# A fused attention and gated feed-forward kernel: early transposes moved to TensorE, loads reordered, one exp phase moved forward, wider weight reads

## The chip, the cores and the metric

The kernel runs on one core of one Trainium2 chip. The metric is device time in microseconds (us). Executions of one kernel agree within about 1%, some are longer; those over 1.5% above the fastest are marked slow. A profile is one execution; its span is about 2 us shorter than the device time of the same execution.

PE is the matrix engine (TensorE), which writes its results to a memory of its own, PSUM; PEld is its weight loads, DVE the vector engine, ACT the scalar engine (exp, log, sine), POOL issues the loads from memory, SP the DMA transposes and the stores.

## The reference

```python
q, k, v: (8, 8, 576, 64)   p: (8, 8, 32, 64)   w_in: (512, 2048)   w_out: (2048, 512)
def sm_attn(qq, kk, vv):                       # softmax(scale * qq kk^T) vv
p_packed = sm_attn(p, k, v)                    # 32 packed rows per batch and head
out = sm_attn(q, p_packed, p_packed)
x = out.transpose(0, 2, 1, 3).reshape(4608, 512)
h = x @ w_in;  y = (h * cos(h)) @ w_out        # y is the result, float32
```

## The kernel before

The kernel works batch by batch, in a software pipeline. For batch `b` there are these pieces, each with its name in the profile:

- `s1` (matmul of transposed k against p), its exp on ACT, and `pp` (packed values); `s2` (transposed q), its exp, `sums` and `normalise` (result `a2n`);
- `ppw`: the packed values times `w_in`, kept as `PPW`; then h (`hT`, with the 64 rows left over of each batch in `ht`), its cosine on ACT (`cosT`), the product on DVE (`gT`, `joint`);
- the output matmuls `ot`, which serve as filler for PE while ACT and DVE work.

Slot `s` of the main loop does h of batch `s`, the output of batch `s-1`, and attention for `s+1` and `s+2`. ACT needs one function table for exp and log and another for sine (1.28 us for each switch), so the exps of a slot are gathered into one exp phase. The parts that the argument touches:

```python
    def load(n, b):                                  # from memory, cast to bf16
        t = x[n, b] = ld_pool.tile([KP, H, KC * D], BF16, ...)
        G.dma_start(out=t, in_=src[n][b].rearrange("h (p c) d -> p h (c d)", c=KC))
    def dma_T(n, b):                                 # transpose by DMA
        t, f = T_tile(n, b)
        nc.sync.dma_start_transpose(out=t, in_=f)
    def pe_T(n, b, engs):                            # transpose by PE, copied out of PSUM
        t, f = T_tile(n, b)
        for i in range(3):
            ps = work.tile([128, 8, KP], BF16, name="tps", tag="w")
            for j in range(8):
                nc.tensor.transpose(ps[:, j, :], f[:, (8*i+j)*128:(8*i+j+1)*128], ident[0:KP, 0:KP])
            copy(engs[i % len(engs)], t[:, 8*i:8*i+8, :], ps)
    # ... (cut)
    # loads in program order: k0 v0 q0, w_in (512 columns), w_in (the rest), p, w_out x4,
    #                         k1 q1 v1, k2 q2 v2
    # ... batch 0 by pe_T: s1, pp, s2, ppw, sums, normalise
    dma_T("k", 1)
    dma_T("q", 1)
    for fc in range(NFC):                            # slot 0: h of batch 0, nothing else
        if fc % 4 == 2 and fc < 12:
            ppw_piece(0, fc // 4 + 1, [V, A])
        h_mm(0, fc)
        run(h_sin(0, fc))
    dup_p(2, 16, V); pack_p(1, 4); pack_p(4, 8)
    dma_T("k", 2)
    set_filler(0)                                    # middle phase: attention of batches 1 and 2
    exp_table()
    fill(16)                                         # 16 output matmuls of batch 0
    for i in range(3): s1_mm(1, i); s1_exp(1, i)
    fill(12)
    pp_piece(1)
    # ... s2(1), ppw(1), s1(2), sums(1), normalise(1), pp(2), 16 more output matmuls
    for s in range(1, B):                            # slots 1 to 7
        # ... load(s+2); dma_T("k", s+2); h in two halves with an exp phase between; dma_T("q", s+2)
```

The softmax here doesn't subtract the row's maximum and nothing guards it: scores larger than these inputs give would overflow.

Of the kernel before, what the change touches and what calls it, by code (L numbers as in the profile page):

```python
# [8 lines left out]
FP32 = mybir.dt.float32  # L9
# [7 lines left out]
def kernel(  # L17
# [54 lines left out]
    a1T = const.tile([KP, KC, 2, 4, 32], BF16, name="a1T")  # L72
    src = {"k": k, "q": q, "v": v}
# [16 lines left out]
    def copy(eng, out, in_):  # L90
        if eng is A:
            A.copy(out=out, in_=in_)  # L92
        else:
            eng.tensor_copy(out=out, in_=in_)  # L94


    def T_tile(n, b):
        t = xT[n, b] = T_pool.tile([128, H * KC // 2, KP], BF16, name=n + "T", tag=n + "T")
        return t, x[n, b].rearrange("p h x -> p (h x)")
# [5 lines left out]
    def pe_T(n, b, engs):  # L105
        t, f = T_tile(n, b)
        for i in range(3):
            ps = work.tile([128, 8, KP], BF16, name="tps", tag="w")
            for j in range(8):
                nc.tensor.transpose(ps[:, j, :], f[:, (8 * i + j) * 128:(8 * i + j + 1) * 128], ident[0:KP, 0:KP])  # L110
            copy(engs[i % len(engs)], t[:, 8 * i:8 * i + 8, :], ps)

# [17 lines left out]
    def s1_mm(b, i):  # L130

        ps = s1_ps[b, i] = work.tile([KP, 2, 2, 4, 32], FP32, name="s1", tag="w")
        for h in range(H):
            nc.tensor.matmul(ps[:, :, h % 2, h // 2, :], xT["k", b][:, h * (KC // 2) + i, :],  # L134
                             P2[:, b, h], start=True, stop=True)

    def s1_exp(b, i):
        ps = s1_ps.pop((b, i))
        A.activation(out=a1T[:, 2 * i:2 * i + 2].rearrange("p c o a n -> p (c o a n)"),  # L139
                     in_=ps.rearrange("p c o a n -> p (c o a n)"), func=AF.Exp, scale=scale)  # L140
# [23 lines left out]
    def ppw_piece(b, n, engs):  # L164
        if b not in PPW:
            PPW[b] = ppw_pool.tile([128, 2, DF], BF16, name="PPW", tag="PPW")
        ps = [work.tile([128, 512], FP32, name="ppw", tag="w") for _ in range(2)]
        for hp in range(4):
            for o in range(2):
                r = slice(64 * o, 64 * o + 64)  # L170
                nc.tensor.matmul(ps[o][32 * hp:32 * hp + 32], ppT[b][r, 2 * hp + o, :],  # L171
                                 w_in_bf[r, hp, n * 512:(n + 1) * 512], start=True, stop=True,
                                 tile_position=(64 * o, 32 * hp))
        for g in range(2):
            dst = PPW[b][:, g, n * 512:(n + 1) * 512]
            s = rinv[b][:, 2 * g:2 * g + 1]
            if engs[g] is A:
                A.activation(out=dst, in_=ps[g], func=AF.Copy, scale=s)  # L178
            else:
                engs[g].tensor_scalar(out=dst, in0=ps[g], scalar1=s, scalar2=None, op0=ALU.mult)  # L180

    def s2_mm(b, g):

        ps = s2_ps[b, g] = [work.tile([128, S // 2], FP32, name="s2", tag="w") for _ in range(2)]
        for hp in range(4):
            for o in range(2):
                r = slice(64 * o, 64 * o + 64)
                h = 2 * hp + g
                nc.tensor.matmul(ps[o][32 * hp:32 * hp + 32], ppT[b][r, h, :],
                                 xT["q", b][r, 3 * h:3 * h + 3, :].rearrange("p c t -> p (c t)"),  # L190
                                 start=True, stop=True, tile_position=(64 * o, 32 * hp))
# [114 lines left out]
    def run(todo):  # L306
        for f in todo:
            f()
# [3 lines left out]
    nc.sync.dma_start(out=p_raw[:, 0:2, :], in_=p_rows[:, 0:2, :])  # L312
# [4 lines left out]
    load_w_in(512, DF)  # L317
    G.dma_start(out=p_raw[:, 2:, :], in_=p_rows[:, 2:, :])
    for n in range(4):
        load_w_out(n)  # L320
    for b in (1, 2):
        for n in "kqv":
            load(n, b)
    exp_table()
    V.memset(P2[:, 0], 0.0)
# [4 lines left out]
    for j in range(4):  # L330
        V.memset(ones_blk[j * 32:(j + 1) * 32, j * 32:(j + 1) * 32], 1.0)

    def dup_p(a, b, eng):
        for t in range(2):
            eng.tensor_copy(out=p_bf[:, a:b, t, :], in_=p_raw[:, a:b, :])

    dup_p(0, 2, V)
    pack_p(0, 1)
# [5 lines left out]
    V.memset(P2[:, 1:], 0.0)  # L344
# [4 lines left out]
    ppw_piece(0, 0, [V, V])  # L349
    for i in range(3):  # L350
        sums(0, i)
    normalise(0)
    dma_T("k", 1)
    dma_T("q", 1)


    for fc in range(NFC):
        if fc % 4 == 2 and fc < 12:
            ppw_piece(0, fc // 4 + 1, [V, A])
        h_mm(0, fc)  # L360
        run(h_sin(0, fc))
    dup_p(2, 16, V)
    pack_p(1, 4)
    pack_p(4, 8)
    dma_T("k", 2)


    set_filler(0)
    exp_table()
    fill(16)  # L370
# [3 lines left out]
    fill(12)  # L374
    pp_piece(1)
    for g in range(2):
        s2_mm(1, g)
        s2_exp(1, g)
    ppw_piece(1, 0, [V, V])
    fill(4)  # L380
    for i in range(3):
        s1_mm(2, i)
        s1_exp(2, i)
        sums(1, i)
        fill(2)
    normalise(1)
    dma_T("q", 2)
    for n in range(1, 4):
        ppw_piece(1, n, [V, A])
        fill(2)  # L390
    pp_piece(2)
    for n in "kqv":
        load(n, 3)
# [16 lines left out]
    def exp_phase(s, b2, b1):  # L410
        exp_table()
        s2_exp(b2, 0)
        s2_mm(b2, 1)
        s2_exp(b2, 1)
        fill(3)
        for i in range(3):
            if b1 is not None:
                s1_mm(b1, i)
                s1_exp(b1, i)
            fill(4)  # L420
        for i in range(3):
            sums(b2, i)
            fill(2)
        normalise(b2)
        h_mm(s, 8)
        fill(3)
        h_mm(s, 9)
        fill(3)

    for s in range(1, B):  # L430
        if s > 1:
            set_filler(s - 1)
        n1, n2 = s + 1 < B, s + 2 < B
        if s > 1 and n2:
            for n in "kqv":
                load(n, s + 2)
        if n2:
            dma_T("k", s + 2)
        before = {}
        if n1:  # L440
            before[1] = [lambda: ppw_piece(s + 1, 0, [V, A])]
            before[3] = [lambda: ppw_piece(s + 1, 1, [V, A])]
            before[7] = [lambda: s2_mm(s + 1, 0)]
            before[11] = [lambda: ppw_piece(s + 1, 2, [V, A])]
            before[13] = [lambda: ppw_piece(s + 1, 3, [V, A])]
        if n2:
            before[9] = [lambda: pp_piece(s + 2)]
        rest = filler[1] - (27 if n1 else 0)
        h_steps(s, range(0, 8), before, rest // 2)
        if n1:  # L450
            exp_phase(s, s + 1, s + 2 if n2 else None)
        if n2:
            dma_T("q", s + 2)
        h_steps(s, range(8, 16), before, filler[1])
        fill(100)
# [32 lines left out]
```

## Time and profile before

| | us |
|---|---|
| device time, median of 3 (range) | 290.17 (289.23 to 291.49) |
| the profiled execution, marked slow | 299.3, span 297.1 |

The first view is the table of windows of the kernel before: the stretch in us from the span's start, its length, then the busy time of each engine with its number of instructions, PE's granted clock (1 is full), the DMA share and GB/s.

```profile
core 0: us, PE busy (x) PEld busy (x) DVE busy (x) ACT busy (x) POOL busy (x), PEclk, DMA share, GB/s
40.00:110.00 70.00, 48.55 (x492) 24.59 (x500) 27.16 (x52) 33.11 (x55) 5.37 (x7) 0.76 1.30 161
110.00:160.00 50.00, 48.88 (x469) 25.73 (x475) 29.74 (x49) 40.99 (x66) 4.60 (x6) 1.00 0.90 150
160.00:220.00 60.00, 59.19 (x567) 31.57 (x573) 39.07 (x70) 48.35 (x78) 1.53 (x2) 1.00 0.57 103
220.00:280.00 60.00, 59.48 (x383) 29.63 (x390) 37.22 (x57) 41.18 (x64) 0.00 (x0) 1.00 0.19 49
```

From 110 us on PE is busy 98 to 99% of the time at full clock: this part is bound by PE. From 40 to 110 us PE is busy 48.55 of 70 us at a mean clock of 0.76, ACT is not even half busy, and the DMA share is 1.30. The start is bound by something else. The chain of waits (the work that ended last, followed back from the end), by engine and by line, says what:

```profile
PE 65%; DMA 30%; ACT 1%; issue 1%; POOL 1%; DVE 1%; POOLq 0%; ACTq 0%
PE ot L280 38%; DMA kT<-k_bf 19%; PE hT L235 15%; DMA k_bf<-in_k_dram 8%; DMA q_bf<-in_q_dram 3%; PE ppw L171 3%; PE ht L242 2%; PE pp L148 1%; PE sm L208 1%; PE pp L153 1%; ACT osb L92 0%; DVE ppT L160 0%; ACT lns L209 0%; POOL k_bf L81 0%
```

Its longest pieces in the start, each with its start, length and what it was:

```profile
13.54 24.68 DMA k_bf<-in_k_dram
38.23 17.67 DMA kT<-k_bf
...
57.15 17.14 DMA kT<-k_bf
...
80.09 12.80 DMA kT<-k_bf
```

The load of k1, then the DMA transposes of k1, k2 and k3, stand on the chain one after another. The list of waits agrees (engine and what was waited for: us in total, times, longest):

```profile
PE s_590 L134 <- DMA kT<-k_bf: 9.1, 1, 9.1
...
PE s_747 L134 <- DMA kT<-k_bf: 5.8, 1, 5.8
```

### The profile page before, as it was taken

To read this page: it belongs to the slowest core of one execution; us is meant where nothing else is said; L and a number is where in the kernel's file an instruction comes from. 1 tells how busy PE (TensorE), PEld (TensorE's weight loads), DVE (VectorE), ACT (ScalarE), POOL (GpSimd) and SP (SyncE) were. 2 spreads that over 40 slices of the span, in tenths; PEclk is the share of its full clock that TensorE was granted. 3 is DMA by queue.
4 is the path that set the end of the run, shared out by engine and by line. 5 is a ranking of instruction groups with operands and counts; after the bars stand their busy time and mean duration, and the time that the engine had idled before them with its cause. 6 is when DMAs were issued, how large, how long until landed. Compare 5 with 4: busy or idle time off the path is not lost.

```text
span 297.1 us, 5419 instructions
## 1 busy us (share of the span) xinstructions
PE 252.2 (85%) x2197; PEld 131.3 (44%) x2232; DVE 157.5 (53%) x276; ACT 188.8 (64%) x298; POOL 24.0 (8%) x37
## 2 busy tenths in 40 slices
PE   0957753492987799999999999999999999999994
PEld 0823421330554435554545455545554445545441
DVE  2266980011095487276826862778198727665210
ACT  1358940211689976967798879778978797655200
POOL 8313100120103003002011000000000000000000
PEclk9999979575699969999999999999999999999999
DMA  7999999999999999928988981725351112112222
GB/s 107 205 216 230 205 192 191 179 143 170 118 95 169 227 143 156 182 58 116 215 143 161 164 153 36 105 62 103 75 113 35 38 35 73 35 35 73 71 71 71
DMA packets 59335, 36.91 MB, mean 124 GB/s; under 512 B 34624, under 2 KB 53568, under 8 KB 59312
## 3 DMA queue, kind: packets, MB, share of 16 engines
q0 software_dynamic: 20576, 18.81, 41.8%
q1 hardware_dynamic: 38736, 17.77, 35.2%
q8 instruction: 17, 0.28, 0.4%
q14 instruction: 6, 0.05, 0.0%
HBM read 37.22 MB, written 9.44 MB: 157 GB/s over the span
## 4 chain that ended last, share of the span: by engine, by line
PE 65%; DMA 30%; ACT 1%; issue 1%; POOL 1%; DVE 1%; POOLq 0%; ACTq 0%
PE ot L280 38%; DMA kT<-k_bf 19%; PE hT L235 15%; DMA k_bf<-in_k_dram 8%; DMA q_bf<-in_q_dram 3%; PE ppw L171 3%; PE ht L242 2%; PE pp L148 1%; PE sm L208 1%; PE pp L153 1%; ACT osb L92 0%; DVE ppT L160 0%; ACT lns L209 0%; POOL k_bf L81 0%; PE s_590 L134 0%
## 5 line engine op out<-in xcount | busy, mean ns | idle before, releaser
L280 PE MATMUL ot<-w_out_bf,gT 128*128 128x512 bf16 x487 | 134.0, 392 | 2.0 <-issue 1.0
L249 ACT ACTIVATE cosT<-hT,pihalf 128x512 bf16<-128x512 f32 x128 | 85.7, 689 | 35.7 <-PE hT L235 32.5
L250 DVE TENSOR_TENSOR gT<-hT,cosT 128x512 bf16<-128x512 f32 x128 | 86.0, 685 | 29.2 <-ACT cosT L249 29.0
L235 PE MATMUL hT<-a2n,PPW 128*128 128x512 bf16 x249 | 76.7, 394 | 4.4 <-DVE a2n L215 2.7
L280 PEld LDWEIGHTS <-gT 128*128 128x128 bf16 x512 | 44.9, 101 | 45.3 <-issue 10.2
L235 PEld LDWEIGHTS <-PPW 128*128 128x128 bf16 x256 | 27.3, 115 | 30.0 <-issue 3.4
L215 DVE TENSOR_TENSOR a2n<-a2u,lns 128x576 bf16<-128x576 bf16 x16 | 11.4, 755 | 46.9 <-ACT lns L213 46.9
L242 PEld LDWEIGHTS <-PPW 128*128 128x128 bf16 x256 | 24.4, 116 | 21.6 <-issue 3.0
L180 DVE TENSOR_SCALAR PPW<-ppw,rinv 128x512 bf16<-128x512 f32 x34 | 25.0, 746 | 5.9 <-PE ppw L171 5.8
L242 PE MATMUL ht<-a2n,PPW 128*128 128x64 bf16 x256 | 24.4, 199 | 0.2
L134 PEld LDWEIGHTS <-kT 128*96 128x96 bf16 x192 | 14.2, 150 | 22.5 <-DMA kT<-k_bf 18.4
L94 DVE COPY osb<-ot 128x512 f32<-128x512 f32 x18 | 12.3, 684 | 21.2 <-PE ot L280 21.2
L92 ACT COPY osb<-ot 128x512 f32<-128x512 f32 x18 | 10.6, 587 | 18.0 <-PE ot L280 17.8
L178 ACT ACTIVATE PPW<-ppw,rinv 128x512 bf16<-128x512 f32 x30 | 20.4, 684 | 1.6 <-PE ppw L171 1.6
L160 DVE CAST ppT<-pp 64x128 bf16<-64x128 f32 x32 | 9.2, 287 | 20.9 <-PE pp L153 20.4
L171 PE MATMUL ppw<-w_in_bf,ppT 64*32 64x512 bf16 x256 | 16.8, 420 | 3.3 <-DVE gT L250 1.3
L280 PE MATMUL ot<-w_out_bf,joint 128*128 128x512 bf16 x61 | 15.8, 380 | 0.5 <-issue 0.5
L209 ACT ACTIVATE lns<-sm 128x384 f32<-128x384 f32 x24 | 11.5, 490 | 2.7 <-PE sm L208 1.5
L81 POOL DMA_DIRECT2D q_bf<-in_q_dram x8 | 6.2, 772 | 72.9 <-DMA qT<-q_bf 52.1
L139 ACT ACTIVATE a1T<-s_590 96x512 bf16<-96x512 f32 x1 | 0.6, 592 | 16.7 <-PE s_590 L134 16.7
L254 ACT ACTIVATE cosTt<-ht,pihalf 128x512 bf16<-128x512 f32 x16 | 10.9, 684 | 0.0
L256 DVE TENSOR_TENSOR joint<-ht,cosTt 128x512 bf16<-128x512 f32 x16 | 10.9, 680 | 0.0
(154 smaller groups left out, 173.4 us busy)
## 6 DMA issues: line engine op xcount, KB each, us to landing
k_bf<-in_k_dram POOLq DMA_DIRECT2D x8, 576.0 KB, 12.6
v_bf<-in_v_dram POOLq DMA_DIRECT2D x8, 576.0 KB, 10.3
q_bf<-in_q_dram POOLq DMA_DIRECT2D x8, 576.0 KB, 8.4
out_dram<-osb SPq DMA_DIRECT2D x24, 192.0 KB, 2.2
out_dram<-osb SPq DMA_DIRECT2D x24, 128.0 KB, 2.4
w_out_bf<-in_moe_w_out_dram POOLq DMA_DIRECT2D x4, 512.0 KB, 23.8
w_in_bf<-in_moe_w_in_dram POOLq DMA_DIRECT2D x1, 1536.0 KB, 18.9
out_dram<-osb SPq DMA_DIRECT2D x24, 64.0 KB, 2.0
```

Of the source, the lines that this page charges most:

```text
L94: eng.tensor_copy(out=out, in_=in_)
L134: nc.tensor.matmul(ps[:, :, h % 2, h // 2, :], xT["k", b][:, h * (KC // 2) + i, :], P2[:, b, h], start=True, stop=True)
L171: nc.tensor.matmul(ps[o][32 * hp:32 * hp + 32], ppT[b][r, 2 * hp + o, :], w_in_bf[r, hp, n * 512:(n + 1) * 512], start=True, stop=True, ti ...
L178: A.activation(out=dst, in_=ps[g], func=AF.Copy, scale=s)
L180: engs[g].tensor_scalar(out=dst, in0=ps[g], scalar1=s, scalar2=None, op0=ALU.mult)
L209: A.activation(out=lns[b].rearrange("p g s -> p (g s)")[:, c], in_=ps, func=AF.Ln)
L215: V.tensor_tensor(out=a2n[b][:, g], in0=a2u[b][:, g], in1=lns[b][:, g], op=ALU.mult)
L235: nc.tensor.matmul(ps, h_lhs(b, g, fc), a2n[b][:, g, 0:512], start=(g == 0), stop=(g == 1))
L242: nc.tensor.matmul(ht[b][:, jj, :], h_lhs(b, g, fc - j + jj), a2n[b][:, g, 512:576], start=(g == 0), stop=(g == 1))
L249: A.activation(out=cs, in_=ps, func=AF.Sin, bias=pihalf)
L250: todo = [lambda: V.tensor_tensor(out=gT[b][:, fc, :], in0=ps, in1=cs, op=ALU.mult)]
L280: nc.tensor.matmul(ps, t[:, fc, x0:x0 + 128], w_out_bf[:, fc, :], start=(fc == 0), stop=(fc == NFC - 1))
```

## The change

It has four parts: k1, q1, k2, q2 and k3 are transposed by PE in place of DMA; the loads come in the order of their use, with k1 among the chunks of `w_in`; the middle phase is gone, and its exps go ahead of slot 0 (`s1` of batch 1) and into an exp phase inside slot 0, so that output matmuls of batch 0 are all left for slot 1; and `s1` reads 128 columns of transposed k in place of 96 (the 32 rows too many are never read). With the schedule goes a smaller thing: p is copied and packed in parts, earlier, and partly by POOL. Cut to its core:

```diff
+    kTs = [const.tile([128, H * S // 2 + 32], BF16, name=f"kT{i}") for i in range(2)]
-        ps = s1_ps[b, i] = work.tile([KP, 2, 2, 4, 32], FP32, name="s1", tag="w")
+        ps = s1_ps[b, i] = work.tile([128, 2, 2, 4, 32], FP32, name="s1", tag="w")
-            nc.tensor.matmul(ps[:, :, h % 2, h // 2, :], xT["k", b][:, h * (KC // 2) + i, :],
+            nc.tensor.matmul(ps[:, :, h % 2, h // 2, :], xT["k", b][:, x0:x0 + 128],
 ...
     load_w_in(0, 512)
-    load_w_in(512, DF)
-    (p, w_out x4, then k, q, v of batches 1 and 2)
+    load("k", 1)
+    for n in range(1, 4):
+        load_w_in(512 * n, 512 * n + 512)
+    (v1, q1, k2, p, w_out x4, v2, q2, k3, v3, q3)
 ...
+    pe_T("k", 1, [V])
     normalise(0)
-    dma_T("k", 1)
-    dma_T("q", 1)
+    for i in range(3): s1_mm(1, i); s1_exp(1, i)
-    (slot 0 as h alone; the middle phase)
 ...
     def exp_phase(s, fc, b2, b1):
         exp_table()
         s2_exp(b2, 0)
-        s2_mm(b2, 1)
         s2_exp(b2, 1)
-        fill(3)
+        fill(6)
+        if s == 0:
+            pe_T("k", 2, [V, A, V])
         (s1 and its exps of b1, sums and normalise of b2, with fillers between)
-    for s in range(1, B):
+    for s in range(B):
+        if s == 0:
+            mid = 12                       # the exp phase of slot 0 comes after 12 of 16 h blocks
+            (ppw(0), pp_piece(1), pe_T("q", 1, [A, V, A]), ppw(1) between the h blocks)
+        if s == 1:
+            (pp_piece(2), pack_p, pe_T("q", 2, [V, A, V]), pe_T("k", 3, [V, A, V]))
+        before[mid - 1] += [lambda: s2_mm(s + 1, 0), lambda: s2_mm(s + 1, 1)]
```

More of the change, by code (lines that the diff above doesn't have):

```diff
@@ L97, in T_tile @@
     def T_tile(n, b):
-        t = xT[n, b] = T_pool.tile([128, H * KC // 2, KP], BF16, name=n + "T", tag=n + "T")
-        return t, x[n, b].rearrange("p h x -> p (h x)")
+        t = kTs[b % 2] if n == "k" else T_pool.tile([128, H * S // 2], BF16, name=n + "T", tag=n + "T")
+        xT[n, b] = t
+        return t[:, 0:H * S // 2].rearrange("p (j t) -> p j t", t=KP), x[n, b].rearrange("p h x -> p (h x)")
     def dma_T(n, b):
@@ L103, in dma_T, with pe_T @@
         nc.sync.dma_start_transpose(out=t, in_=f)
-    def pe_T(n, b, engs):
-        t, f = T_tile(n, b)
-        for i in range(3):
+    def pe_T(n, b, engs, parts=(0, 1, 2)):
+        if 0 in parts:
+            pe_T.open[n, b] = T_tile(n, b)
+        t, f = pe_T.open[n, b]
+        for i in parts:
             ps = work.tile([128, 8, KP], BF16, name="tps", tag="w")
@@ L111, in pe_T @@
             copy(engs[i % len(engs)], t[:, 8 * i:8 * i + 8, :], ps)
+    pe_T.open = {}
     def pack_p(b0, b1):
@@ L130, in s1_mm @@
     def s1_mm(b, i):
-        ps = s1_ps[b, i] = work.tile([KP, 2, 2, 4, 32], FP32, name="s1", tag="w")
+        ps = s1_ps[b, i] = work.tile([128, 2, 2, 4, 32], FP32, name="s1", tag="w")
         for h in range(H):
-            nc.tensor.matmul(ps[:, :, h % 2, h // 2, :], xT["k", b][:, h * (KC // 2) + i, :],
+            x0 = (h * (KC // 2) + i) * KP
+            nc.tensor.matmul(ps[:, :, h % 2, h // 2, :], xT["k", b][:, x0:x0 + 128],
                              P2[:, b, h], start=True, stop=True)
@@ L139, in s1_exp @@
         A.activation(out=a1T[:, 2 * i:2 * i + 2].rearrange("p c o a n -> p (c o a n)"),
-                     in_=ps.rearrange("p c o a n -> p (c o a n)"), func=AF.Exp, scale=scale)
+                     in_=ps[0:KP].rearrange("p c o a n -> p (c o a n)"), func=AF.Exp, scale=scale)
     def pp_piece(b):
@@ L162, in pp_piece, with ppw_piece @@
         V.reciprocal(rinv[b], ps[:, 128:132])
-    def ppw_piece(b, n, engs):
+    def ppw_piece(b, ns, engs):
         if b not in PPW:
             PPW[b] = ppw_pool.tile([128, 2, DF], BF16, name="PPW", tag="PPW")
-        ps = [work.tile([128, 512], FP32, name="ppw", tag="w") for _ in range(2)]
-        for hp in range(4):
-            for o in range(2):
-                r = slice(64 * o, 64 * o + 64)
-                nc.tensor.matmul(ps[o][32 * hp:32 * hp + 32], ppT[b][r, 2 * hp + o, :],
-                                 w_in_bf[r, hp, n * 512:(n + 1) * 512], start=True, stop=True,
-                                 tile_position=(64 * o, 32 * hp))
-        for g in range(2):
-            dst = PPW[b][:, g, n * 512:(n + 1) * 512]
-            s = rinv[b][:, 2 * g:2 * g + 1]
-            if engs[g] is A:
-                A.activation(out=dst, in_=ps[g], func=AF.Copy, scale=s)
-            else:
-                engs[g].tensor_scalar(out=dst, in0=ps[g], scalar1=s, scalar2=None, op0=ALU.mult)
+        opened = []
+        for n in ns:
+            ps = [work.tile([128, 512], FP32, name="ppw", tag="w") for _ in range(2)]
+            opened.append((n, ps))
+            for hp in range(4):
+                for o in range(2):
+                    r = slice(64 * o, 64 * o + 64)
+                    nc.tensor.matmul(ps[o][32 * hp:32 * hp + 32], ppT[b][r, 2 * hp + o, :],
+                                     w_in_bf[r, hp, n * 512:(n + 1) * 512], start=True, stop=True,
+                                     tile_position=(64 * o, 32 * hp))
+        for n, ps in opened:
+            for g in range(2):
+                dst = PPW[b][:, g, n * 512:(n + 1) * 512]
+                s = rinv[b][:, 2 * g:2 * g + 1]
+                if engs[g] is A:
+                    A.activation(out=dst, in_=ps[g], func=AF.Copy, scale=s)
+                else:
+                    engs[g].tensor_scalar(out=dst, in0=ps[g], scalar1=s, scalar2=None, op0=ALU.mult)
     def s2_mm(b, g):
@@ L189, in s2_mm @@
                 nc.tensor.matmul(ps[o][32 * hp:32 * hp + 32], ppT[b][r, h, :],
-                                 xT["q", b][r, 3 * h:3 * h + 3, :].rearrange("p c t -> p (c t)"),
+                                 xT["q", b][r, h * (S // 2):(h + 1) * (S // 2)],
                                  start=True, stop=True, tile_position=(64 * o, 32 * hp))
@@ L311 @@
     load("k", 0)
-    nc.sync.dma_start(out=p_raw[:, 0:2, :], in_=p_rows[:, 0:2, :])
+    nc.sync.dma_start(out=p_raw[:, 0:6, :], in_=p_rows[:, 0:6, :])
     make_identity(nc, ident)
@@ L316, with dup_p @@
     load_w_in(0, 512)
-    load_w_in(512, DF)
-    G.dma_start(out=p_raw[:, 2:, :], in_=p_rows[:, 2:, :])
+    load("k", 1)
+    for n in range(1, 4):
+        load_w_in(512 * n, 512 * n + 512)
+    load("v", 1)
+    load("q", 1)
+    load("k", 2)
+    G.dma_start(out=p_raw[:, 6:, :], in_=p_rows[:, 6:, :])
     for n in range(4):
         load_w_out(n)
-    for b in (1, 2):
-        for n in "kqv":
-            load(n, b)
+    load("v", 2)
+    load("q", 2)
+    load("k", 3)
+    def dup_p(a, b, eng):
+        for t in range(2):
+            eng.tensor_copy(out=p_bf[:, a:b, t, :], in_=p_raw[:, a:b, :])
+    dup_p(6, 16, G)
+    load("v", 3)
+    load("q", 3)
     exp_table()
-    V.memset(P2[:, 0], 0.0)
+    V.memset(P2[:, 0:3], 0.0)
     V.memset(pihalf, PI_HALF)
@@ L331 @@
         V.memset(ones_blk[j * 32:(j + 1) * 32, j * 32:(j + 1) * 32], 1.0)
-    def dup_p(a, b, eng):
-        for t in range(2):
-            eng.tensor_copy(out=p_bf[:, a:b, t, :], in_=p_raw[:, a:b, :])
-    dup_p(0, 2, V)
-    pack_p(0, 1)
+    for t in kTs:
+        V.memset(t[:, H * S // 2:], 0.0)
+    dup_p(0, 6, V)
+    pack_p(0, 3)
+    V.memset(P2[:, 3:], 0.0)
     pe_T("k", 0, [V, A])
@@ L343 @@
     pp_piece(0)
-    V.memset(P2[:, 1:], 0.0)
     pe_T("q", 0, [V, A])
@@ L348 @@
         s2_exp(0, g)
-    ppw_piece(0, 0, [V, V])
+    ppw_piece(0, [0], [V, V])
     for i in range(3):
         sums(0, i)
+    pe_T("k", 1, [V])
     normalise(0)
-    dma_T("k", 1)
-    dma_T("q", 1)
-    for fc in range(NFC):
-        if fc % 4 == 2 and fc < 12:
-            ppw_piece(0, fc // 4 + 1, [V, A])
-        h_mm(0, fc)
-        run(h_sin(0, fc))
-    dup_p(2, 16, V)
-    pack_p(1, 4)
-    pack_p(4, 8)
-    dma_T("k", 2)
-    set_filler(0)
-    exp_table()
-    fill(16)
     for i in range(3):
@@ L373 @@
         s1_exp(1, i)
-    fill(12)
-    pp_piece(1)
-    for g in range(2):
-        s2_mm(1, g)
-        s2_exp(1, g)
-    ppw_piece(1, 0, [V, V])
-    fill(4)
-    for i in range(3):
-        s1_mm(2, i)
-        s1_exp(2, i)
-        sums(1, i)
-        fill(2)
-    normalise(1)
-    dma_T("q", 2)
-    for n in range(1, 4):
-        ppw_piece(1, n, [V, A])
-        fill(2)
-    pp_piece(2)
-    for n in "kqv":
-        load(n, 3)
     def h_steps(b, fcs, before, n_fill):
@@ L408, in h_steps, with exp_phase @@
             n_f = want
-    def exp_phase(s, b2, b1):
+    def exp_phase(s, fc, b2, b1):
         exp_table()
         s2_exp(b2, 0)
-        s2_mm(b2, 1)
         s2_exp(b2, 1)
-        fill(3)
+        fill(6)
+        if s == 0:
+            pe_T("k", 2, [V, A, V])
         for i in range(3):
@@ L419, in exp_phase @@
                 s1_exp(b1, i)
-            fill(4)
+            fill(3)
         for i in range(3):
@@ L424, in exp_phase @@
         normalise(b2)
-        h_mm(s, 8)
-        fill(3)
-        h_mm(s, 9)
-        fill(3)
-    for s in range(1, B):
-        if s > 1:
-            set_filler(s - 1)
+        if fc < NFC:
+            h_mm(s, fc)
+            fill(3)
+            h_mm(s, fc + 1)
+            fill(3)
+    for s in range(B):
+        set_filler(s - 1)
         n1, n2 = s + 1 < B, s + 2 < B
@@ L436 @@
                 load(n, s + 2)
-        if n2:
             dma_T("k", s + 2)
-        before = {}
-        if n1:
-            before[1] = [lambda: ppw_piece(s + 1, 0, [V, A])]
-            before[3] = [lambda: ppw_piece(s + 1, 1, [V, A])]
-            before[7] = [lambda: s2_mm(s + 1, 0)]
-            before[11] = [lambda: ppw_piece(s + 1, 2, [V, A])]
-            before[13] = [lambda: ppw_piece(s + 1, 3, [V, A])]
-        if n2:
-            before[9] = [lambda: pp_piece(s + 2)]
+        before = {fc: [] for fc in range(NFC)}
+        mid = 8
+        if s == 0:
+            mid = 12
+            for n in range(1, 4):
+                before[4 * n - 3].append(lambda n=n: ppw_piece(0, [n], [V, A]))
+            before[8].append(lambda: pp_piece(1))
+            before[10].append(lambda: pe_T("q", 1, [A, V, A]))
+            before[11].append(lambda: ppw_piece(1, [0], [A, V]))
+            before[13].append(lambda: ppw_piece(1, [1], [V, A]))
+            before[14].append(lambda: ppw_piece(1, [2], [V, A]))
+            before[15].append(lambda: ppw_piece(1, [3], [V, A]))
+        elif n1:
+            before[1].append(lambda: ppw_piece(s + 1, [0], [V, A]))
+            before[3].append(lambda: ppw_piece(s + 1, [1], [V, A]))
+            before[11].append(lambda: ppw_piece(s + 1, [2], [V, A]))
+            before[13].append(lambda: ppw_piece(s + 1, [3], [V, A]))
+        if s == 1:
+            before[0].append(lambda: pp_piece(2))
+            before[4].append(lambda: pack_p(3, 5))
+            before[5].append(lambda: pe_T("q", 2, [V, A, V]))
+            before[6].append(lambda: pe_T("k", 3, [V, A, V]))
+            before[12].append(lambda: pack_p(5, 8))
+        if n1:
+            before[mid - 1] += [lambda: s2_mm(s + 1, 0), lambda: s2_mm(s + 1, 1)]
+        if s > 0 and n2:
+            before[9].append(lambda: pp_piece(s + 2))
         rest = filler[1] - (27 if n1 else 0)
-        h_steps(s, range(0, 8), before, rest // 2)
+        h_steps(s, range(0, mid), before, max(rest // 2, 0))
         if n1:
-            exp_phase(s, s + 1, s + 2 if n2 else None)
-        if n2:
+            exp_phase(s, mid, s + 1, s + 2 if n2 else None)
+        if s > 0 and n2:
             dma_T("q", s + 2)
-        h_steps(s, range(8, 16), before, filler[1])
+        h_steps(s, range(mid, NFC), before, filler[1])
         fill(100)
```

## The prediction

> **What bounds the kernel now.** Two regimes. By the table of windows, from 110 us to the end PE is 98 to 99% busy in every 30 us stretch, at full granted clock: PE-bound, about 29 us per slot (the `pp` work of slots 2 to 5 starts at 129.7, 159.0, 188.0, 216.6 in the chain of waits). Before 110 us PE is not the limit: it is busy 72 of 110 us, at a granted clock of 0.76 from 40 to 110, and the DMA share there is 1.3. The chain runs through DMA: k1 loads from 13.5 to 38.2, its transpose to 55.9, that of k2 from 57.2 to 74.3, k3's from 80.1 to 92.9. The waits show PE idle 9.1 and 5.8 us for `kT`; from 38 to 84 us there is no h work at all, only out(0) filler between waits. Slot 2 starts at about 109.4.
>
> The profiled execution was slow (299.3 against 290.17); as the part after 110 us is at full clock, I put the 9 us into the DMA-bound start.
>
> **What the change does.**
> - Removes five of 14 DMA transposes (k1, q1, k2, q2, k3), the early, contended ones (17 us each from issue to landing, 5 to 7 later).
> - Adds on PE 5 x 24 transposes: 24 took 2.1 us cold; I estimate 1.8 warm. Adds 15 PSUM copies of 0.56 (DVE) or 0.80 us (ACT).
> - Loads in order of use: the start moved about 190 GB/s written, so (estimate) k1 lands near 19 us, v1 27, q1 30, k2 33, w_out 46, q2 52, k3 55: each about 3 to 15 us before its use. The start becomes engine-bound.
> - 128-wide weights for the s1 matmuls. The Trainium skill ("TensorE: Matmul & The Clock Gate", weight-path perf modes) says fast weight load needs 128 weights. The trace: 8 loads of 96 columns span 0.61 us warm, about 76 ns each; the 128-wide ones of `pp` sums pace at about 40. Worth about 0.3 us a batch, 1.5 to 2 us in all.
> - Same-page clock gate: the same s1 matmul takes 268 ns before 80 us and 209 after, so short idle remains costly in slot 0.
>
> **Sum, on the critical path.** Slot 0: first cos at 25.0 now; k1's transpose, DVE copies and three exps delay it to about 27. ACT then needs: 16 cos 9.9, 2 cosTt 1.4, 7 `PPW` 4.7, 3 copies 2.4, exp phase with two table loads (2 x 1.28) about 8.5: 27 us, DVE nearly as much; with some 10% of waiting slot 0 ends near 57 (PE 56). Slot 1 is PE-bound: 13.4 us of non-filler work, 64 filler matmuls 13.8, an extra `pp` 1.3, q2, k3 and p transposes 4.3: 33 us. Slot 2 starts near 89 instead of 109 (profiled) or about 100 (fast). The rest, 187.7 us, stays but for 1.5 us of s1. 89 + 186 + 2 (time over span) = 277; I say 276. Nothing off the path (idle POOL, later transposes) is worth time.
>
> **Prediction: 276 us, 268 to 285 in 8 of 10. Faster by over 2%: 0.89; within 2%: 0.08; slower: 0.03.**
>
> **What would show it.** Right: no DMA transpose before about 75 us; chain nearly all PE and ACT; slot 0 with ACT 85% or more busy from 27 to 57; slot 2 (first `ot<-joint`) at 86 to 93; the stretch from there to the end 184 to 188 us; s1 weight loads below 60 ns. Wrong: PE waiting for `k_bf`, `q_bf`, `v_bf` or `w_in_bf` in slot 0; h delayed far past 27.
>
> **What would make it wrong.** Loads later than estimated; PSUM turnover (s2 now takes four of five work buffers at once) stalling PE in slot 0 or in every slot; half clock through all of slot 0; the 9 us not being in the start.

## The result

| | median us (range) | runs |
|---|---|---|
| before | 289.83 (289.23 to 291.49) | 4 |
| changed | 274.34 (272.35 to 274.64) | 4 |

The ratio of fast runs is 0.9443 (95% interval 0.9382 to 0.9503). Ratios here are the mean time of one kernel's fast runs over that of the other's in the same rounds, so they are not quite the ratio of the medians.

The profile before was of a slow execution, so I took one more look at the kernel before among the experiments (289.47 us; this lies within the fast ones). Its windows:

```profile
27.00:40.00 13.00, 9.05 (x75) 4.89 (x74) 12.45 (x21) 12.15 (x20) 1.67 (x3) 1.00 1.17 207
40.00:57.00 17.00, 6.04 (x29) 2.80 (x30) 4.12 (x7) 0.36 (x1) 0.00 (x0) 0.75 1.29 184
57.00:89.00 32.00, 29.00 (x354) 16.03 (x359) 14.76 (x29) 22.90 (x40) 5.37 (x7) 0.92 1.22 189
89.00:110.00 21.00, 18.15 (x186) 9.30 (x188) 16.15 (x28) 16.61 (x25) 2.31 (x3) 0.92 1.25 200
```

The changed kernel's, for the same stretches:

```profile
27.00:40.00 13.00, 10.50 (x162) 6.88 (x161) 11.44 (x23) 10.85 (x19) 4.97 (x7) 0.87 1.23 217
40.00:57.00 17.00, 13.94 (x164) 8.06 (x164) 9.03 (x17) 14.19 (x23) 1.54 (x2) 0.65 1.22 205
57.00:89.00 32.00, 32.00 (x337) 17.41 (x336) 23.23 (x43) 25.92 (x41) 3.85 (x5) 0.97 1.05 167
89.00:110.00 21.00, 21.00 (x220) 11.19 (x218) 11.98 (x22) 16.08 (x27) 0.77 (x1) 1.00 0.73 128
```

From 40 to 57 us the old kernel's ACT worked 0.36 us, the new one's 14.19. From 57 us the new kernel's PE is never idle; the old one reached that state after 100 us. The chain after, answering to the one before:

```profile
PE 82%; ACT 7%; DMA 5%; issue 2%; POOL 1%; DVE 1%; ACTq 0%; POOLq 0%
PE ot L293 47%; PE hT L248 19%; DMA k_bf<-in_k_dram 5%; PE ppw L183 3%; PE ht L255 3%; ACT cosT L262 3%; PE pp L156 2%; PE tps L115 2%; ACT a1T L147 1%; PE sm L221 1%; ACT PPW L191 1%; PE pp L161 1%; ACT L262 1%; ACT a2u L211 1%; DVE gT L26
```

DMA fell from 30% of the chain to 5%. What is left of it is the load of k1, which now lands at 19.8 us in place of 38.2, and the PE transposes follow at once:

```profile
5.05 14.75 DMA k_bf<-in_k_dram
19.85 2.12 PE tps L115 x24
```

As a measure of the whole start I use the first `ot` matmul that reads `joint`, which begins slot 2. It is at 110.0 us in the slow profile before, at 100.3 in the fast one and at 86.5 after the change. From there to the end of the span it is 187.1, 187.0 and 186.3 us. So of 14.4 us of span, 13.7 came from the start and 0.7 from the rest; and all the excess of the slow profile was in the start too.

### The profile page after: what moved, and what is told of

Its sections match the earlier page's. It is cut to its first block, busy times and chain, and to the rows that moved or that the text cites. A ratio compares the mean times of both kernels' runs of the same rounds, so it can differ in the third digit from the quotient of the medians.

```text
span 272.8 us, 5701 instructions
## 1 busy us (share of the span) xinstructions
PE 252.7 (93%) x2352; PEld 135.4 (50%) x2352; DVE 161.2 (59%) x285; ACT 192.3 (70%) x304; POOL 26.8 (10%) x41
## 4 chain that ended last, share of the span: by engine, by line
PE 82%; ACT 7%; DMA 5%; issue 2%; POOL 1%; DVE 1%; ACTq 0%; POOLq 0%
PE ot L293 47%; PE hT L248 19%; DMA k_bf<-in_k_dram 5%; PE ppw L183 3%; PE ht L255 3%; ACT cosT L262 3%; PE pp L156 2%; PE tps L115 2%; ACT a1T L147 1%; PE sm L221 1%; ACT PPW L191 1%; PE pp L161 1%; ACT L262 1%; ACT a2u L211 1%; DVE gT L263 1%
## 5 line engine op out<-in xcount | busy, mean ns | idle before, releaser
L262 ACT ACTIVATE cosT<-hT,pihalf 128x512 bf16<-128x512 f32 x128 | 86.6, 688 | 42.1 <-PE hT L248 37.9
L263 DVE TENSOR_TENSOR gT<-hT,cosT 128x512 bf16<-128x512 f32 x128 | 86.5, 685 | 31.3 <-ACT cosT L262 31.2
L248 PE MATMUL hT<-a2n,PPW 128*128 128x512 bf16 x256 | 79.1, 394 | 2.6 <-DVE gT L263 1.3
L293 PEld LDWEIGHTS <-gT 128*128 128x128 bf16 x512 | 43.3, 98 | 41.0 <-issue 4.3
L248 PEld LDWEIGHTS <-PPW 128*128 128x128 bf16 x256 | 28.5, 115 | 30.5 <-issue 6.3
L255 PEld LDWEIGHTS <-PPW 128*128 128x128 bf16 x256 | 24.3, 116 | 21.1 <-issue 2.4
L255 PE MATMUL ht<-a2n,PPW 128*128 128x64 bf16 x256 | 24.3, 198 | 0.0
L191 ACT ACTIVATE PPW<-ppw,rinv 128x512 bf16<-128x512 f32 x31 | 21.1, 682 | 0.0
L183 PE MATMUL ppw<-w_in_bf,ppT 64*32 64x512 bf16 x256 | 15.1, 414 | 1.9 <-DVE gT L263 1.8
L293 PE MATMUL ot<-w_out_bf,joint 128*128 128x512 bf16 x64 | 16.5, 380 | 0.0
L222 ACT ACTIVATE lns<-sm 128x384 f32<-128x384 f32 x24 | 10.9, 504 | 0.8 <-PE sm L221 0.3
L115 PE MATMUL tps<-ident,k_bf 96*128 96x96 bf16 x96 | 7.3, 255 | 4.4 <-DMA k_bf<-in_k_dram 3.4
L269 DVE TENSOR_TENSOR joint<-ht,cosTt 128x512 bf16<-128x512 f32 x16 | 10.9, 680 | 0.0
L267 ACT ACTIVATE cosTt<-ht,pihalf 128x512 bf16<-128x512 f32 x16 | 10.9, 680 | 0.0
```

Of the source, the lines that this page charges most:

```text
L115: nc.tensor.transpose(ps[:, j, :], f[:, (8 * i + j) * 128:(8 * i + j + 1) * 128], ident[0:KP, 0:KP])
L183: nc.tensor.matmul(ps[o][32 * hp:32 * hp + 32], ppT[b][r, 2 * hp + o, :], w_in_bf[r, hp, n * 512:(n + 1) * 512], start=True, stop=True, ti ...
L191: A.activation(out=dst, in_=ps[g], func=AF.Copy, scale=s)
L222: A.activation(out=lns[b].rearrange("p g s -> p (g s)")[:, c], in_=ps, func=AF.Ln)
L248: nc.tensor.matmul(ps, h_lhs(b, g, fc), a2n[b][:, g, 0:512], start=(g == 0), stop=(g == 1))
L255: nc.tensor.matmul(ht[b][:, jj, :], h_lhs(b, g, fc - j + jj), a2n[b][:, g, 512:576], start=(g == 0), stop=(g == 1))
```

## The experiments

Three theories stood. Theory 1, mine: the DMA transposes, slowed by the loads beside them, were the main cost, and PE transposes bring most of the gain. Theory 2: the late landing of k1 was the cost, and the load order brings the gain. Theory 3: the exp phases inside slot 0 bring it. The first runs apply parts to the kernel before, or take parts away from the changed one.

### The kernel before, unedited

> The kernel before, unedited, for a profile in the fast state, as the profile before was taken at 299.3 us. My prediction put the 9 us of excess into the start: then the span from the first joint out matmul to the end is again 187 us, and that matmul starts at 100 to 103 us in place of 110.0. If the excess lay in the PE-bound part, the first joint matmul stays near 108 to 110 and the rest is shorter than 182 us.

Measured: 289.47 us, first joint matmul at 100.25 us, 187.0 us from there. As expected: the slow execution lost its 9 us in the start.

### PE transposes alone

```diff
 (the kernel before)
-    dma_T("k", 1)
-    dma_T("q", 1)
-    dma_T("k", 2)
+    pe_T("k", 1, [V, A, V])        # ahead of the first 16 fillers of the middle phase
+    pe_T("q", 1, [V, A, V])        # ahead of the next 12
+    pe_T("k", 2, [V, A, V])        # ahead of the next 4; q2 and k3 likewise in slot 1
```

> The kernel before with one part of the change: k1, q1, k2, q2, k3 transposed by PE at their use, old load order, old schedule (exp phases of batches 1 and 2 after slot 0). Theory 1 (the contended DMA transposes on the chain are the main cost): h(0) ends near 39 us as before, then the middle phase is 22 to 26 us of PE and ACT work in place of 45, slot 2 starts near 88 to 93; 278 to 282 us, about two thirds of the gain. Theory 2 (the late landing of k1, near 38 us, is the main cost; the load order brings the gain): hardly faster, 286 us or more. Theory 3 (the exp phases inside slot 0 bring the gain): also 286 or more.

Measured: 284.17 us (281.67 to 287.9; the execution at 287.9 is slow), ratio 0.9741 (0.9654 to 0.9828). The profiled execution (282.71 us) did what theory 1 says: the middle phase lasted from 41.9 to 66.0 us and slot 2 began at 92.9. But the median lies above the range that I expected, and the gain is 2.6% of 5.6%: not two thirds, less than half. The fast executions differ in PE's mean granted clock: 0.993 at 281.67 us, 0.973 at 285.63. The run with spare matmuls, below, comes back to this.

### Load order alone

```diff
 (the kernel before)
     load_w_in(0, 512)
-    load_w_in(512, DF)
-    (p, w_out x4, k1 q1 v1, k2 q2 v2)
+    load("k", 1)
+    for n in range(1, 4): load_w_in(512 * n, 512 * n + 512)
+    (v1 q1 k2, p, w_out x4, v2 q2)
```

> The kernel before with the new load order only, all transposes still by DMA. Theory 1: k1 lands near 20 us, but its transpose then shares the DMA engines with the remaining loads (each transpose again 10 us or more), and the k2 and k3 transposes still stand on the chain; 284 to 290 us. Theory 2: the transposes start 18 us earlier and the whole start moves forward by 10 us or more; 280 us or less. Theory 3: no change, 288 to 291.

Measured: 292.01 us, ratio 1.0043 (0.9981 to 1.0106): no gain, and above the range of every theory; theory 2 is out. The timeline of SP shows why; the second column is the time to issue:

```profile
19.97 8.38 SPq L103 DMA_TRANSPOSE kT<-k_bf  x1
36.54 16.26 SPq L103 DMA_TRANSPOSE qT<-q_bf  x1
52.98 11.70 SPq L103 DMA_TRANSPOSE kT<-k_bf  x1
```

The transpose of k1 begins at 20.0 us in place of 38.3, but now runs beside the whole backlog of loads and lands 19 us later; that of q1 takes 16 us merely to issue and lands at 62.3. On the chain the load of q1 and the transposes of q1 and k2 now stand one after another:

```profile
10.68 25.84 DMA q_bf<-in_q_dram
36.54 16.44 DMA qT<-q_bf
52.98 17.21 DMA kT<-k_bf
```

The Trainium skill ("DMA: Bandwidth & Descriptors", section "Issuing engines are not separate DMA queues") states that DMAs issued by different engines run on the same 16 DMA engines and interleave. This agrees with it: in this run the transposes of k1, q1 and k2, beside the loads and in part beside each other, took 17 to 26 us from issue to landing; in the loop of the changed kernel one takes 5 to 8.

### Load order and PE transposes, old schedule

> The kernel before with the new load order and the PE transposes, but the old schedule. Theory 1: nothing in the middle phase waits for a load any more; equal to the run with PE transposes alone or up to 2 us faster: 277 to 281. Theory 2: clearly faster than PE transposes alone, by 5 us or more. Theory 3: most of the gain is still missing, 284 or more.

The edit is the last two together. Measured: 282.85 us, ratio 0.9724 (0.9646 to 0.9801). It is equal to PE transposes alone within the intervals, as theory 1 expected, yet 8.5 us above the changed kernel, which theory 3 expected; the median lies between the two theories' ranges. No load and no DMA transpose is on the path of the middle phase any more. The window from 40 to 57 us shows what is:

```profile
40.00:57.00 17.00, 14.97 (x198) 9.23 (x198) 8.04 (x17) 4.82 (x9) 2.32 (x3) 0.88 1.20 212
```

From 40 to 57 us ACT works 4.82 of 17 us, while PE runs output matmuls. These matmuls are then missing in slot 1, where ACT is the busier engine (18.63 us of the 20 from 70 to 90, PE 17.64) and PE has gaps. In this execution PE's clock then fell to 0.52 (90 to 97 us) and h matmuls ran at half speed; it took 286.65 us at a mean clock of 0.970, three others took 282.8 at 0.986 (a fifth, slow, 287.85). The run with PE transposes alone, whose profile took 282.7 us and has a shorter dip (0.57 from 89 to 93 us), is the fairer measure: between the first cosine and slot 2 it has 50.6 us of ACT work in 67.6 us. The changed kernel has 49.6 in 60.7. The work of ACT is nearly the same, its idle time is not.

PE is the busier engine over that stretch in both: 58.4 us, and 54.3 at a lower clock in the changed kernel (0.86 against 0.95). What the new schedule does is to let the two overlap. With PE transposes alone, from 39 to 66 us PE works 24.3 of 27 us and ACT 14.1; from 66 to 92.9 ACT works 23.7 of 26.9. I read this from the profiles; no run moves the output matmuls alone. Nor are they all of it: in both runs of the old schedule PE stands for 3.4 us ahead of the middle phase, waiting for DVE to copy p, which the changed kernel does earlier.

### The changed kernel without the new load order

```diff
 (the changed kernel)
-    load("k", 1) ... (the new order)
+    load_w_in(512, DF); (p, w_out x4, k1 q1 v1, k2 q2 v2, k3)
```

> The changed kernel with the old load order (k1 behind all of w_in, p and w_out). All theories: PE stands at the k1 transposes before the first h matmul until k1 lands near 38 us in place of 20, and slot 0 starts about 17 us later; 288 to 292 us. If it is below 284, the wait for k1 is less on the path than the chain after the change says.

Measured: 292.38 us, ratio 1.0073 (1.0002 to 1.0145). The k1 transposes start at 38.2 us in place of 19.85, and everything after them is 18 us later (slot 2 at 104.3 in place of 86.5). PE waits 18.1 us for k1 and for no other load. In the new schedule the landing of k1 counts one for one.

### The changed kernel with DMA transposes

```diff
 (the changed kernel; k1 stays on PE)
+    dma_T("q", 1)
+    dma_T("k", 2)                  # after normalise(0); q2 and k3 at the start of slot 1
-    pe_T("k", 2, [V, A, V]) ... pe_T("q", 1, ...) ... pe_T("q", 2, ...), pe_T("k", 3, ...)
```

> The changed kernel with q1, k2, q2 and k3 transposed by DMA again, issued as early as their loads land; k1 stays on PE. Theory 1: the q1 transpose begins near 33 us amid the loads, takes 10 us or more, and s2 of batch 1, now at 38.9, waits for it, then s1 of batch 2 for k2: 284 to 290 us. Theory 3 (the schedule alone brings the gain): within 2% of the changed kernel, below 279.

Measured: 297.94 us, ratio 1.027 (1.0218 to 1.0322): slower than the kernel before, and further than I expected. The window from 40 to 57 us, and the two waits that hold the core:

```profile
40.00:57.00 17.00, 0.00 (x0) 0.00 (x0) 0.00 (x0) 0.00 (x0) 0.00 (x0) 0.50 1.21 193
```

```profile
PE s L202 <- DMA qT<-q_bf: 21.5, 1, 21.5
...
PE s L142 <- DMA kT<-k_bf: 11.6, 2, 10.6
```

All the engines of the table stand still for 17 us: `s2` of batch 1 waits for the transpose of q1, issued at 33.2 and landed at 57.7, and `s1` of batch 2 for that of k2, landed at 68.9. The old schedule had h of batch 0 complete, and so output matmuls to fill such waits; the new one has none in slot 0.

So the parts are not additive. The order alone brings nothing and PE transposes alone 2.6%; the schedule, with the wide reads, brings 8.5 us more on top of both. With either of them missing it is no faster than the kernel before: without the order within 2% of it (ratio 1.0073), with four of the five transposes back on DMA slower (1.027).

### Narrow reads in the changed kernel

```diff
-        ps = work.tile([128, 2, 2, 4, 32], FP32, name="s1", tag="w")
+        ps = work.tile([KP, 2, 2, 4, 32], FP32, name="s1", tag="w")
-            ... xT["k", b][:, x0:x0 + 128]
+            ... xT["k", b][:, x0:x0 + KP]
```

> The changed kernel with 96-wide reads of the k blocks. My prediction valued the wide reads at 1.5 to 2 us in all. From the two traces: eight s1 matmuls and loads step by 0.34 us warm with 96 columns and 0.23 with 128, and 0.64 against 0.42 cold; 3 groups per batch, so 1.7 us in slots 1 to 5 and up to 1.3 more where slots 0 and 1 stand on them: 276 to 277.5 us. Rival: the stretch from slot 2 on shrank by only 0.8 us, the rest is absorbed in waits: 274.5 to 275.5.

Measured: 274.85 us, ratio 0.9486 (0.944 to 0.9533) against 0.9443 for the changed kernel, in another set of rounds: not resolved in the total. From slot 2 on it is: 188.1 us against 186.3. The weight loads of `s1` in that stretch, first with 96 columns, then with 128 (columns: count, then busy us and mean ns, then idle us):

```profile
L142 PEld LDWEIGHTS <-kT 128*96 128x96 bf16 x96 | 6.1, 124 | 3.1 <-DMA kT<-k_bf 0.8
```

```profile
L142 PEld LDWEIGHTS <-kT_106 128*128 128x128 bf16 x48 | 2.2, 98 | 1.4
L142 PEld LDWEIGHTS <-kT_107 128*128 128x128 bf16 x48 | 2.2, 98 | 1.5 <-DMA kT_107<-k_bf 0.3 <-issue 0.2
```

For the same 96 loads PEld is busy 6.1 us and 2 x 2.2 us: 1.7 us less. The start of this profile was faster: slot 2 began at 84.2 us, with a clock of 0.80 from 40 to 57 us against 0.65. Four of its six executions ran at a mean clock of 0.985 to 0.987, three of the changed kernel's four at 0.964 to 0.971, and that hides the difference in the total. This run also separates the schedule from the reads: it and the old schedule with order and PE transposes both read 96 columns, and stand at 0.9486 and 0.9724.

### Wide reads in the kernel before

> The kernel before with 128-wide reads of the k blocks only. In the traces so far the stretch from the first joint out matmul to the end is 187.0 in the kernel before, 186.3 in the changed one and 188.1 in the changed one with 96-wide reads, so the wide reads should be worth 1.7 to 1.8 us there: 185.2 in this run. In the total: 287.5 to 288.5 us against 289.9, as s1 in the start waits for DMA anyway. Rival (worth nothing, as the medians of the changed kernel with and without differ by only 0.5 us): stretch 187, total within 0.5 us of before.

The edit is that of the change's `kTs`, `x0` and `s1` lines alone. Measured: 288.02 us against 291.73, ratio 0.9877 (0.9828 to 0.9926). From slot 2 on: 185.9 us against 187.0. The profiled execution was slow, so I use only that stretch of it, which lay at 187 in the slow and the fast profile before alike. The direction is confirmed; the size in the stretch is 1.1 us here and 1.8 us in the changed kernel. The medians differ by 3.7 us, more than the stretch explains; the start varies from one execution to the next, and I don't put the rest down to the reads.

### The old order of `s2` and fillers in the loop

```diff
+        if s > 0: s2_mm(b2, 1)     # between the two groups of exps, as before
-        fill(6) ... fill(3)
+        fill(3) ... fill(4)
```

> The changed kernel with the old order of s2 and fillers in the exp phases of slots 1 to 6 (second s2 group after the first exps, so that s2 holds two work buffers at a time, not four). If the new order costs PE time in every slot by holding four of five buffers (187.0 before to 188.1 with 96-wide reads in both), the stretch from slot 2 on drops from 186.3 to 185.2 and the total to about 273.2. Rival: no difference, or slower, as s2 waits for the table load again: 186.3 or more.

Measured: 274.08 us, ratio 0.9399 (0.9362 to 0.9436); from slot 2 on 186.9 us. These runs resolve no difference, so holding four of five PSUM work buffers has no cost that shows. Why the stretch of the changed kernel with narrow reads is 1.1 us longer than that of the kernel before stays open.

### Spare matmuls in slot 0

```diff
+            for _ in range(n):     # where later slots have n fillers, 27 in all; result unread
+                nc.tensor.matmul(ps, ident, w_in_bf[:, 0, 0:512], start=True, stop=True)
```

> The changed kernel with 27 extra 512-column matmuls on PE in slot 0's exp phase, their result unread, in the places where later slots have out matmuls. If slot 0 is held back by PE's half clock (0.65 granted from 40 to 57 us: tps 2.1 us per 24 against 1.0, pairs of h matmuls 1.04 against 0.59), it ends 1 to 3 us earlier: 271.5 to 273.5. If slot 0 is held by ACT there, no change or up to 2 us slower: 274 to 276.5.

Measured: 273.71 us, ratio 0.9439 (0.9404 to 0.9474), the same as the changed kernel's. The windows:

```profile
27.00:40.00 13.00, 9.80 (x169) 6.36 (x169) 12.11 (x23) 11.83 (x19) 4.97 (x7) 1.00 1.22 215
40.00:57.00 17.00, 14.86 (x187) 8.08 (x188) 8.88 (x18) 14.45 (x24) 1.54 (x2) 1.00 1.22 206
```

The clock is full in both windows, where the changed kernel had 0.65 from 40 to 57 us, and ACT does the same: 14.45 us in place of 14.19. From the first to the sixteenth cosine it took 27.4 us against 27.3, and the median lies between the two ranges that I expected. It is tempting to conclude that PE's clock does not hold slot 0. But the run changes two things, the clock and PE's work, and the timelines of ACT, of one profile each, show two effects that cancel:

| run | first cosine to table load, us | table load to next cosine, us | clock, 54 to 58 us | ACT's wait for slot 1's second h block, us | first joint matmul, us |
|---|---|---|---|---|---|
| changed kernel | 14.05 | 9.53 | 0.50 | 2.81 | 86.5 |
| old order of `s2` (slot 0 as in the changed kernel) | 12.92 | 9.41 | 0.50 | 2.73 | 85.7 |
| narrow reads | 12.92 | 9.88 | 1.00 | 0.87 | 84.2 |
| spare matmuls | 12.92 | 10.83 | 1.00 | 0.87 | 85.2 |
| k2 early (below) | 13.88 | 8.06 | 0.50 | 2.85 | 86.1 |
| three small things (below) | 13.88 | 8.05 | 1.00 | 0.87 | 83.6 |

With spare matmuls ACT reaches the exp phase 1.1 us sooner than in the profile of the changed kernel, where PE had 0.50 of its clock from 34.9 to 38.2 us. In the exp phase it loses 1.3 us: it waits four times (1.2 us in all, against once, 0.7 us), three of them for matmuls that stand behind spare ones. At the start of slot 1 the wait is short in the three profiles whose clock was 1.00 there and about 2 us longer in the three at 0.50:

```profile
57.74 0.69 ACT L262 ACTIVATE cosT<-hT,pihalf 128x512 bf16<-128x512 f32 x1 [2.81 <-PE hT L248]
```

```profile
56.12 0.69 ACT L262 ACTIVATE cosT<-hT,pihalf 128x512 bf16<-128x512 f32 x1 [0.87 <-PE hT L248]
```

The first line is of the changed kernel, the second of this run. The totals fit: the changed kernel took 272.35 us in its execution at a mean clock of 0.983 and 274.1 to 274.6 in the three at 0.964 to 0.971, and the narrow reads (273.9 to 275.1 at 0.985 and more, 276.3 and 277.2 below) and the old order of `s2` (272.7 and 273.1 at 0.989, 273.9 to 275.1 below) fall into two groups likewise. So, by the timelines and by these groups, PE's clock costs up to about 2 us; no run shows it in a total, as none changes the clock alone.

### k2 transposed ahead of the exp phase, copied by DVE

```diff
-        if s == 0:
-            pe_T("k", 2, [V, A, V])                        # in the exp phase
+            before[11].append(lambda: pe_T("k", 2, [V]))   # before it, copies on DVE
```

> The changed kernel with the k2 transposes of slot 0 ahead of the exp phase and all three copies on DVE: ACT loses a copy of 0.8 us and a wait of 0.66 us in the exp phase, PE work is unchanged. If slot 0 is bound by ACT there (as the run with spare matmuls says), the time from the first to the sixteenth cos shrinks from 27.3 to 26 to 26.8 us and the total by 0.5 to 1.3: 273 to 273.8. If not ACT but the order on PE or the DVE queue binds, no change or slower: 274.3 to 275.5.

Measured: 272.62 us (271.23 to 274.38), ratio 0.935 (0.9305 to 0.9395); the run with the old order of `s2`, in the same rounds, had 274.08 and 0.9399. The timeline of ACT in the exp phase of slot 0, first in the changed kernel, then here:

```profile
39.91 1.28 ACT L231 ACT_TABLE_LOAD   x1
...
42.75 0.81 ACT L93 COPY kT_106<-tps 128x768 bf16<-128x768 bf16 x1
44.22 0.59 ACT L147 ACTIVATE a1T<-s_750 96x512 bf16<-96x512 f32 x1 [0.66 <-PE s_750 L142]
...
48.14 1.28 ACT L262 ACT_TABLE_LOAD   x1
49.44 1.26 ACT L262 ACTIVATE cosT<-hT,pihalf 128x512 bf16<-128x512 f32 x2
```

```profile
40.60 1.28 ACT L231 ACT_TABLE_LOAD   x1
41.90 1.68 ACT L211 ACTIVATE a2u<-s,rinv 128x288 bf16<-128x288 f32 x4
43.45 1.56 ACT L147 ACTIVATE a1T<-s 96x512 bf16<-96x512 f32 x3
...
47.36 1.28 ACT L262 ACT_TABLE_LOAD   x1
48.66 1.27 ACT L262 ACTIVATE cosT<-hT,pihalf 128x512 bf16<-128x512 f32 x2
```

From table load to first cosine it was 9.53 us and is 8.06: the copy of 0.81 and the wait of 0.66 us before the `s1` exps are gone. Of these 8.06 us ACT works 7.98, so its own work sets the length of this exp phase here. First to sixteenth cosine is 25.6 us against 27.3, but the old order of `s2`, with slot 0 as in the changed kernel, has 26.0: most of the 1.7 us is a difference between executions. ACT also waits 0.86 us more ahead of the exp phase, for `ppw` matmuls. The median is below the range that I expected, but the intervals of the two runs overlap, so a gain in the total is not shown.

### A version that adds three small things

```diff
+ (the early k2 of the last run)
+ (ten spare matmuls after h_mm(0, 13), at the end of slot 0's exp phase)
+ (last output chunk: copied in halves by DVE and ACT; some of the last stores from ACT's queue)
```

> The changed kernel with k2 transposed early on DVE copies, ten spare matmuls at the end of slot 0's exp phase so that PE does not enter slot 1 at half clock (pairs of h matmuls took 1.04 us there against 0.59), and the last output chunk copied by DVE and ACT in halves and stored from two queues. Expected from the parts: ratio to before 0.935 for the early k2 alone, 0.5 to 1 us less from the clock, 0.3 to 0.6 from the tail: 271 to 272.5 us, ratio 0.930 to 0.934 to the kernel before. If the spare matmuls only cost PE time, 272.6 to 273.5.

Measured: 271.86 us (271.38 to 272.75), ratio 0.9372 (0.9344 to 0.94). It beats the kernel before by 6.3%, and its median is 2.5 us below that of the changed kernel (other rounds; the intervals of the two ratios just overlap). The ratio lies above the 0.930 to 0.934 that I expected, and against the early k2 alone the intervals overlap, so the spare matmuls and the tail are not shown to help in the total. In the profiles slot 2 began at 83.6 us against 86.1, and the table above shows where: the clock is 1.00 at the start of slot 1 in place of 0.50, and ACT waits 0.87 us in place of 2.85. From slot 2 on it took 186.5 against 186.2, so the tail shows no gain there.

## Why the prediction was right, and where it was not

Predicted were 276 us (268 to 285), and 274.34 were measured.

- **Two regimes, and the 9 us of the slow profile in the start.** Right: slot 2 at 110.0 in the slow and 100.3 in the fast profile, the rest 187.1 and 187.0.
- **No DMA transpose before about 75 us.** Right: the first is at 74.7.
- **First cosine near 27 us.** 25.86.
- **Slot 0 ends near 57, PE at 56.** Right: the first output matmul is at 55.8. ACT was to be 85% busy from 27 to 57 us; it was 10.85 + 14.19 of 30 us, 83%.
- **Slot 1 takes 33 us.** The mis-sized term: it took 30.7 (55.8 to 86.5), PE-bound as said. I had 1.8 us for 24 warm transposes (warm: at full clock; cold: at half). Measured in the timeline of PE, cold (granted clock 0.50), then warm, with what follows each:

```profile
35.75 2.11 PE L115 MATMUL tps<-ident,q_bf 96*128 96x96 bf16 x24
37.65 0.93 PE L248 MATMUL hT<-a2n,PPW 128*128 128x512 bf16 x2
...
63.22 1.19 PE L115 MATMUL tps<-ident,q_bf 96*128 96x96 bf16 x24
64.24 0.60 PE L293 MATMUL ot<-w_out_bf,gT 128*128 128x512 bf16 x2
```

Warm, the next matmul starts 1.02 us after 24 transposes do, 43 ns each; cold, 1.90 us, 79 ns each. Two sets of 24 in slot 1, each 0.8 us shorter than I had, are 1.6 of the 2.3 us. The Trainium skill ("TensorE: Matmul & The Clock Gate", "Part 4: PE-mode transpose") gives about 275 ns for one; single instructions here last 202 to 282 ns too, but they overlap, and the pace is what counts.
- **Slot 2 at 86 to 93 us, 89 in the sum.** 86.5.
- **Loads 3 to 15 us ahead of use.** Right for k2, q2, k3 and w_out (47.7, used at 55.8); less for q1 (33.3, used at 35.8) and v1 (30.4, used at 31.7); wrong for k1, which landed at 19.8 and was awaited for 0.2 us.
- **Wide reads worth 1.5 to 2 us, loads below 60 ns.** The reason held: the Trainium skill (same page, "Weight-path perf modes") says fast weight load is on when the number of weights is 128. Eight loads span 0.49 us in place of 0.61, 61 ns each, just above the 60. In the kernel 1.1 to 1.8 us; but the stretch as a whole shrank by 0.7, as something that I have not found added 1.1. The size was in part luck: my own figures, 76 against 40 ns for the 24 loads of a batch, give 0.9 us a batch, not the 0.3 that I wrote and that was about measured.
- **Short idle remains costly in slot 0 because of the clock.** The profiles agree: at half clock ACT waits about 2 us longer at the start of slot 1. The run with the clock held at full was no shorter, as its spare matmuls cost about what the clock saved.

What the prediction did not say, and theory 1 made of it, fell: that the DMA transposes taken off the chain are the gain. They are a condition of it. Less than half comes from them alone; with their waits gone, the start is a matter of overlapping about 50 us of ACT's work with PE's 54 to 58. The old schedule overlaps them less, as its profiles show; which part of the schedule brings how much was not tested.

## What to carry to other kernels

When a transfer on the chain is slowed by others beside it, starting it earlier among them may move nothing, as here; moving it to an engine with room brought 2.6%. After a wait is taken away, ask which engine has the most work in that stretch and whether the order of the program keeps it fed: here the schedule gave as much as the removed waits. A probe that adds work to an engine to keep its clock up also takes that engine's time: before an equal total is read as no effect, look in the timeline for two that cancel. And a schedule that pulls work forward has less to fill a wait with, so try the parts of such a change together before dropping one that shows nothing alone.

## What the Trainium skill lacked or had wrong

- "DMA: Bandwidth & Descriptors", section "DMA Transpose (X-bar)": it has no duration for a transpose. The page's section "Latency and other measured facts" has an effective bandwidth of 261 GB/s for one, which is 2.3 us (estimate) for the 96 x 3072 bf16 transposes here. They landed 5 to 8 us after issue in the loop, and 17 to 26 us after it beside a backlog of loads; then one also took SP up to 16.3 us to issue.
- "TensorE: Matmul & The Clock Gate", "Part 4": it gives the time of one transpose (about 275 ns) and no pace for a series of them (elsewhere the page has a pace for matmuls in general): 43 ns warm, 79 ns cold, for 96 x 128 blocks. It says that the full clock does not engage for transposes; between other matmuls they ran at the warm pace here.
- The same page, "Why this matters for your kernels": it recommends avoiding idle gaps of PE over about 3 us. That was not enough here: in slot 0 of the changed kernel the clock fell to 0.50 three times, though PE's longest gap there was 1.8 us; from 24 to 34.9 us, ahead of the first fall, PE was busy 8.35 of 10.9 us with no gap over 1.2. (The page does mention oscillation from short gaps elsewhere.)
- The same page, "Weight-path perf modes": it gives about 2x measured for fast weight load. For `s1`, with a 64-column matmul after each load, eight loads went from 0.61 to 0.49 us; but these were 96 columns against 128, so the two factors are not the same thing.
